# Compressive memory of 32 heads as 32x32 blocks of head pairs, with q and k rows ordered pair by pair

## The chip, the cores and the metric

The kernel runs on one core of a Trainium2 chip. It uses five instruction engines: PE (TensorE, the matmuls; PEld is its weight load), DVE (VectorE), ACT (ScalarE), POOL (GpSimd) and SP (SyncE, which here does nothing but issue DMAs, in the order of the program). The metric is the device time of one execution in microseconds. Three executions of the kernel before took 783.08, 779.81 and 781.45 us, median 781.45 us.

## What is computed

One transformer block on x of 2048 rows and 512 features, with a LayerNorm whose scale and shift come from a condition vector ahead of each half. The first half is an attention with 32 heads of 16 features that walks over four segments of 512 rows; inside a segment it is causal softmax attention, and across segments each head carries a 16x16 memory matrix M and a 16-vector z. The second half is a feed-forward net (512 to 1792 to 512, GELU). The part that the change touches, cut from the reference:

```python
phi = lambda t: jnp.where(t > 0, t + 1.0, jnp.exp(t))
for s in range(N):                       # N = 4 segments
    qs, ks, vs = q[:, :, s], k[:, :, s], v[:, :, s]
    logits = jnp.einsum("bhqd,bhkd->bhqk", qs, ks) * scale + mask
    a_dot = jnp.einsum("bhqk,bhkd->bhqd", _softmax(logits, axis=-1), vs)
    pq = phi(qs)
    num = jnp.einsum("bhld,bhde->bhle", pq, M)
    den = jnp.einsum("bhld,bhd->bhl", pq, z)[..., None] + 1e-6
    outs.append(g * num / den + (1.0 - g) * a_dot)
    pk = phi(ks)
    M = M + jnp.einsum("bhld,bhle->bhde", pk, vs)
    z = z + jnp.einsum("bhld->bhd", pk)
```

## The kernel before

Everything is float32. Where a product has to run at the fast rate, an operand is split into a high and a low part in the reduced type (f32r) and the product takes three matmuls.

The program has three stages. **Projections** (0 to about 177 us of the profiled span): for each segment s = 0 to 3 the normalised rows are transposed (`a_turn`, line 160, names At), scaled (ACT, Ah), split by DVE into Ahh and Ahl (lines 138 and 139), and multiplied by wq, wk and wv: four groups of 128 feature rows for q (12 matmuls of 128x512 each, line 334), four for k, and four blocks of 128 rows for v (12 matmuls each, line 485). **Attention** (to about 475 us): for each head, S units (line 649) whose masked maximum DVE takes (line 637), T units (line 723), exponentials on ACT, and products with V (line 751). **Feed-forward net** (to the end). The first S and T units start while v of segment 3 is still being projected.

The order of the work in the projections is written by hand, as a list of tokens for each segment (`PRM['A']`), and no scheduler changes it. Q0 to Q3, K0 to K3 and V0 to V3 are the projections; R is `mem_read`, U `mem_update`, Ro and Rz `mem_out`, Rs `mem_store`, Rb `mem_load`, At, Ah and H make the next segment's transposed and split input, Tk and Tc transpose the rows of phi(k) and copy them out, and B fills the first two stacks (below). The list of segment 2 reads:

```python
'Q0 Ro s0 D D Q1 s1 D D Q2 s2 Q3 E s3 r K0 Es p0 K1 El p1 K2 p2 K3 R V0 p3 V1 Rs V2 Rb Tk Tc V3 At Ah H U Rn'
```

Segment 1 has the same shape, segment 0 has no R, and segment 3 ends with "... K2 R K3 Rz Rs" and has no U. All PSUM tiles of this stage (`pst`) come in turn from one pool of eight banks, so that a matmul also waits for the last reader of the tile that was allocated eight tiles earlier.

**A group** is 128 feature rows of q or k, which are 8 heads of 16 features. `head_rows` permutes the columns of wq and wk so that row r of a group is feature r // 8 of head r % 8. The heads of a group are thus interleaved, and a product of two heads that don't belong together has to be masked away.

**The memory.** `mem_update` (token U) forms, for each group g, the full 128x128 product of phi(k) and v over the segment's 512 rows: 16 matmuls of 128x128 (line 434, tile mp), of which the mask `mbd` keeps one eighth (line 440), and adds M of the segment before (line 443). `mem_read` (token R) forms the denominators with four matmuls of 32 columns (line 449, tile dn), their reciprocal on DVE (lines 451 to 453, tile rd), and the numerators with four matmuls of 128x512, one per group (line 457, tiles nu), each copied from PSUM by ACT into a tile am (line 459). `mem_store` (line 465) writes rd to DRAM, `mem_load` reads it back broadcast (rb), POOL multiplies am by rb, and `mem_out` (line 480) writes the four am tiles of a segment to DRAM (AMD). In segment 3 the am tiles are written unmultiplied.

**The stacks.** `proj` leaves each group's q or k as two f32r parts in SBUF, and `store` (line 502) writes them to DRAM: the part that is needed twice as one DMA of 512 KB with a broadcast source, the other as one of 256 KB. QD and KD are laid out as [part 3, feature 16, head 8, 512]. `load_stacks` (line 193) reads them back, two heads at a time, as 48 rows (3 parts by 16 features) of 1024 numbers, which lie 16 KB apart in DRAM: for a quarter of heads, Q, two loads for k (kst) and two for q (qst). The first two Q are loaded by token B, in segment 3.

**Queues.** All of these DMAs are issued by SP, strictly in the order of the program. Each DMA waits for one of eight completion semaphores (DMAHW0 to DMAHW7, taken in turn), that is, for the landing of the DMA eight before it on SP's list, beside the waits for its data.

Of the kernel before, what the change touches and what calls it, by code (L numbers as in the profile page):

```python
# [8 lines left out]
F32 = mybir.dt.float32  # L9
# [3 lines left out]
ALU = mybir.AluOpType  # L13
# [9 lines left out]
VW = 17  # L23
# [81 lines left out]
def block_kernel(ctx: ExitStack, tc: tile.TileContext, x, wq, wk, wv, wo, betaq, betam,  # L105
# [56 lines left out]

    QD = [[dram.tile([3, 16, 8, 512], F32, name=f"QD{s}_{g}") for g in range(4)] for s in range(NSEG)]
    KD = [[dram.tile([3, 16, 8, 512], F32, name=f"KD{s}_{g}") for g in range(4)] for s in range(NSEG)]
    TERMS = {"q": (slice(0, 3, 2), slice(1, 2)), "k": (slice(0, 2), slice(2, 3))}
    def home(Q):
# [19 lines left out]
    def load_stacks(Q):  # L186
        s, g, t = Q // 8, (Q // 2) % 4, Q % 2
        for st, dd in ((kst[home(Q)], KD), (qst[home(Q)], QD)):
            rows = dd[s][g].rearrange("c r e n -> (c r) e n")
            for h in range(2):  # L190
                o = 4 * t + 2 * h
                if len(st) == 3:
                    sp.dma_start(st[2][64 * h:64 * h + 48], rows[:, o:o + 2, :])
                else:
                    for p in range(2):
                        sp.dma_start(st[p][64 * h:64 * h + 48], rows[:, o + p, :])
# [26 lines left out]
    with ExitStack() as pa:  # L223
# [4 lines left out]
        def pst(name):  # L228
            return pp.tile([128, 512], F32, tag="ps", name=name)
# [47 lines left out]
        load_x(1)  # L277
        mbd = wp.tile([128, 128], F32, name="mbd")
        m8 = wp.tile([128, 32], F32, name="m8")
# [146 lines left out]
        def mem_update(s):  # L426
            z = zss[s]
            if mem["z"] is not None:
                v.tensor_tensor(out=z, in0=mem["z"], in1=z, op=ALU.add)
            mp = pst(f"mp{s}")  # L430
            for g in range(4):
                for b in range(4):
                    rhs = V[4 * s + b][:, VW * 8 * g:VW * 8 * g + VW * 8].rearrange("p (h c) -> p h c", c=VW)[:, :, :16]
                    pe.matmul(mp[:, 128 * g:128 * g + 128], pks[s][b][:, 128 * g:128 * g + 128], rhs,
                              start=(b == 0), stop=(b == 3))
# [4 lines left out]
            v.tensor_tensor(out=M, in0=mp.rearrange("p (g n) -> p g n", g=4),  # L440
                            in1=mbd[:, :].unsqueeze(1).to_broadcast([128, 4, 128]), op=ALU.mult)
            if mem["M"] is not None:
                v.tensor_tensor(out=M, in0=M, in1=mem["M"], op=ALU.add)
            mem["M"], mem["z"], mem["zm"] = M, z, zm

        def mem_read(s):
            dn = pst(f"dn{s}")
            for g in range(4):
                pe.matmul(dn[32 * g:32 * g + 32, :], mem["zm"][:, g, :], phq[s, g], start=True, stop=True)
            rd = sa.tile([128, 512], F32, tag="rd", bufs=1, name=f"rd{s}")  # L450
            v.tensor_scalar(rd, dn, 1e-6, None, op0=ALU.add)
            v.reciprocal(out=rd, in_=rd)
            v.tensor_scalar(rd, rd, gm[:, 0:1], None, op0=ALU.mult)
            ams = []
            for g in range(4):
                ps = pst(f"nu{s}_{g}")
                pe.matmul(ps, mem["M"][:, g, :], phq[s, g], start=True, stop=True)
                am = sat("am" if s < 3 else "phk", f"am{s}_{g}")
                act.activation(am, ps, AF.Copy)
                ams.append(am)  # L460
            mrd[s] = [rd, ams, []]

        def mem_store(s):
            rdd = dram.tile([128, 512], F32, name=f"rdd{s}")
            sp.dma_start(rdd, mrd[s][0])
            mrd[s][0] = mem["r"] = rdd

        def mem_load(s):
            for g in range(4):
                rb = sat("pkt", f"rb{s}_{g}")  # L470
                sp.dma_start(rb, mrd[s][0][32 * g:32 * g + 8, :].unsqueeze(1).to_broadcast([8, 16, 512]))
                mrd[s][2].append(rb)
# [5 lines left out]
        def mem_out(s):  # L478
            for g, am in enumerate(mrd[s][1]):
                sp.dma_start(AMD[s][g], am)  # L480

# [973 lines left out]
```

## Time and profile before

| what | before |
|---|---|
| median of three executions | 781.45 us (779.81 to 783.08) |
| the execution with the profile | 786.26 us |
| its span in the trace | 784.5 us |
| busy, DVE | 564.9 us (72%) |
| busy, ACT | 456.6 us (58%) |
| busy, POOL | 258.1 us (33%) |

The span runs from the first to the last instruction of the trace; the 1.8 us between it and the execution's own time lie before and behind it. Every position below, such as "at 80 us", counts from the start of the span. In the trace a float32 matmul of the program appears as two records, so the 16 matmuls of `mem_update` are 32 records on PE.

### The profile page before, as it was taken

How to read it: one execution, taken by the hardware profiler on the slowest of the kernel's cores; microseconds unless marked ns; L12 is line 12 of the kernel's file. 1: busy time of each engine (PE TensorE's matmuls, PEld its weight loads, DVE VectorE, ACT ScalarE, POOL GpSimd, SP SyncE). 2: the span in 40 equal slices, each digit the busy share in tenths (PEclk: the TensorE clock that was granted, in tenths of full speed). 3: DMA queues.
4: the chain of work that ended last, by engine and by line, in shares of the span. 5: the costliest groups of instructions: out<-in, count | busy, mean ns of one | idle time of the engine just before them, and what ended most of it. 6: DMA issues, size and time to landing. Idle time of an engine off the chain costs nothing.

```text
span 784.5 us, 14474 instructions
## 1 busy us (share of the span) xinstructions
PE 773.5 (99%) x4532; PEld 541.2 (69%) x4532; DVE 564.9 (72%) x1686; ACT 456.6 (58%) x918; POOL 258.1 (33%) x437
## 2 busy tenths in 40 slices
PE   9999999999999999999999999999999999999998
PEld 4887787866555445555555547788878888888887
DVE  6765696449999889999988889868569764432424
ACT  3543444443888667777788676767644446652221
POOL 2205143410468445566665662242000404200000
PEclk9999999999999779999999999999999999999999
DMA  9777755396587677878777755595676524545543
GB/s 337 268 258 262 281 213 200 144 315 196 136 195 183 164 169 185 228 206 228 185 201 209 214 167 158 195 303 177 201 232 207 191 94 163 173 147 167 172 127 115
DMA packets 97376, 156.28 MB, mean 199 GB/s; under 512 B 15552, under 2 KB 31296, under 8 KB 97300
## 3 DMA queue, kind: packets, MB, share of 16 engines
q1 hardware_dynamic: 96436, 153.79, 63.6%
q10 hardware_dynamic: 864, 1.57, 0.6%
q8 instruction: 36, 0.59, 0.3%
q14 instruction: 40, 0.33, 0.1%
HBM read 93.95 MB, written 60.83 MB: 197 GB/s over the span
## 4 chain that ended last, share of the span: by engine, by line
PE 83%; DVE 5%; DMA 5%; ACT 3%; issue 2%; SPq 1%; POOL 0%; ACTq 0%; DVEq 0%; POOLq 0%
PE bx L1102 9%; PE att L723 8%; PE pv L751 7%; PE att L649 5%; PE q L334 5%; PE bx L1372 5%; PE bv L1102 5%; PE k L334 5%; PE by L1372 4%; PE bv L1372 4%; PE v L485 4%; PE mm L839 4%; PE spare L1372 2%; PE by L1102 2%; PE mm L751 2%
## 5 line engine op out<-in xcount | busy, mean ns | idle before, releaser
L637 DVE CUSTOM_DVE_ANT_0 dump<-att,maskb 128x512 bf16<-128x512 f32 (+3 forms) x512 | 220.2, 487 | 22.5 <-PE att L649 12.9
L723 PE MATMUL att<-qst,kst 50*128 50x512 f32 (+3 forms) x512 | 137.2, 378 | 2.6 <-DVE nm L637 2.2
L649 PE MATMUL att<-kst,qst 48*128 48x512 f32 (+3 forms) x512 | 122.7, 352 | 0.1
L723 PEld LDWEIGHTS att<-qst,kst 50*128 50x128 f32 x512 | 79.5, 191 | 62.1 <-DVE nm L637 47.6
L649 PEld LDWEIGHTS att<-kst,qst 48*128 48x128 f32 x512 | 77.7, 192 | 19.5 <-ACT ptc L726 8.5
L726 ACT ACTIVATE pta<-att 128x512 f32<-128x512 f32 x128 | 69.2, 592 | 32.2 <-PE att L723 25.1
L726 ACT ACTIVATE ptb<-att 128x384 f32<-128x384 f32 x128 | 62.9, 492 | 23.8 <-PE att L649 18.2
L883 POOL TENSOR_TENSOR wb<-wa 128x256 f32<-128x256 f32 x24 | 20.3, 847 | 152.4 <-DMA wa<-in_w 152.4
L708 POOL TENSOR_SCALAR_AFFINE_SELECT pta<-pta 128x256 f32<-128x256 f32 x64 | 27.2, 425 | 104.2 <-ACT pta L726 102.4
L726 ACT ACTIVATE ptc<-att 128x384 f32<-128x384 f32 x128 | 57.2, 492 | 0.9 <-PE att L723 0.9
L139 DVE TENSOR_TENSOR gl<-s,gh 128x512 fp32r<-128x512 f32 x34 | 24.1, 708 | 43.0 <-ACT gh L136 42.9
L708 POOL TENSOR_SCALAR_AFFINE_SELECT ptc<-ptc 128x256 f32<-128x256 f32 x128 | 52.0, 422 | 1.6 <-ACT ptc L726 0.5
L136 ACT ACTIVATE gh<-s 128x512 fp32r<-128x512 f32 x34 | 21.3, 628 | 47.7 <-DMA s<-GD 15.9
L1107 ACT ACTIVATE s<-s,b1t 128x512 f32<-128x512 f32 x42 | 30.3, 722 | 21.5 <-DVE s L1111 21.5
L1111 DVE TENSOR_TENSOR s<-bv,s 128x512 f32<-128x512 f32 x28 | 19.3, 689 | 32.1 <-PE bv L1102 22.3
L637 DVE DVE_READ_ACCUMULATOR2_ANT nm<- 128x1 f32 x512 | 42.2, 82 | 0.0
L708 POOL TENSOR_SCALAR_AFFINE_SELECT ptb<-ptb 128x256 f32<-128x256 f32 x64 | 26.9, 420 | 34.7 <-ACT ptb L726 34.7
L520 POOL TENSOR_SCALAR qp<-qp 128x512 f32<-128x512 f32 x12 | 18.5, 1546 | 42.9 <-ACT qp L515 42.9
L751 PE MATMUL pv<-pta,V 128*32 128x512 f32 x208 | 29.4, 639 | 0.5 <-ACT ms L130 0.5
L139 DVE TENSOR_TENSOR w1ml<-s,w1mh 128x512 fp32r<-128x512 f32 x18 | 13.0, 720 | 21.9 <-ACT w1mh L136 21.9
L751 PE MATMUL pv<-ptc,V 128*32 128x256 f32 (+1 forms) x416 | 28.1, 344 | 0.0
L136 ACT ACTIVATE w1mh<-s 128x512 fp32r<-128x512 f32 x18 | 11.3, 629 | 26.0 <-PE spare L1372 11.6
(378 smaller groups left out, 2078.7 us busy)
## 6 DMA issues: line engine op xcount, KB each, us to landing
GD<-s SPq DMA_DIRECT2D x56, 256.0 KB
s<-GD SPq DMA_DIRECT2D x52, 256.0 KB
kst<-KD SPq DMA_DIRECT2D x58, 192.0 KB
qst<-QD SPq DMA_DIRECT2D x58, 192.0 KB
QD<-q SPq DMA_DIRECT2D x16, 512.0 KB
KD<-k SPq DMA_DIRECT2D x16, 512.0 KB
TD<-ts SPq DMA_DIRECT2D x32, 256.0 KB
xt<-X2D SPq DMA_DIRECT2D x28, 256.0 KB
```

The source lines that it names most:

```text
L136: act.activation(hi, src, AF.Copy)
L139: lo_eng.tensor_tensor(out=lo, in0=src, in1=hi.bitcast(F32), op=ALU.subtract)
L334: pe.matmul(ps, a[:, k, 128 * g:128 * g + 128], b[k], start=(k == 0 and i == 0), stop=(k == KB - 1 and i == 2))
L485: pe.matmul(ps, a[k][:, 128 * b:128 * b + 128], w[:, k, :], start=(k == 0 and i == 0), stop=(k == KB - 1 and i == 2))
L637: v.tensor_tensor_reduce(out=dump[n_dump[0] % 2][:, :n], in0=src, in1=maskb[:, 512 - n:], scale=-1.0, scalar=-4 * NEG, op0=ALU.add, op1=AL ...
L649: pe.matmul(ps[:, o:o + n], q[:, 128 * i:128 * i + 128], k[:, :n], start=True, stop=True)
L708: pool.affine_select(out=t, in_=t, pattern=pattern, compare_op=ALU.is_ge, fill=0.0, base=0, channel_multiplier=-1)
L723: pe.matmul(ps[:, o:o + n], k[:, 128 * j:128 * j + 128], q[:, 128 * j:], start=True, stop=True)
L726: act.activation(pt[:, h, :], ps[:, :m], AF.Exp, scale=0.25)
L751: pe.matmul(ps[32 * c:32 * c + 32, lo:hi], V[4 * s + j][:, VW * hd:VW * hd + 32], pt[:, c // 2, lo - o:hi - o], start=start, stop=stop)
L1102: pe.matmul(ps, a[:, i, k, :], b[k], start=start and k == 0 and c == 0, stop=k == 1 and c == 2, skip_group_check=not start)
L1372: pe.matmul(ps, a[:, c], w[:, lo:hi], start=(f == 0 and i == 0), stop=(last and i == 2))
```

## The change

The row order in a group becomes pair by pair: 32 rows hold two heads, row 2 f + e of them being feature f of head e of the pair. The block of M that matters is then the 32x32 block on the diagonal of each pair, and only these are formed. In `mem_update` 16 matmuls of 128x128 become 64 of 32x32, each still over the 128 rows of one block b; in `mem_read` four matmuls of 128x512 become 16 with 32 rows and 32 columns by 512, placed by `tile_position`, and the tiles nu now hold pair r of all four groups instead of group g. The four PSUM banks of nu are allocated ahead of the matmuls, and ACT copies them after all sixteen. `mbd`, M and the two DVE operations on M shrink to a quarter.

The DRAM layout becomes [pair 4, feature 16, part 3, head 2, 512]. A load of two heads reads one contiguous piece of 192 KB, again as 48 rows of 1024; a store becomes three DMAs of 256 KB with runs of 4 KB at a distance of 12 KB, where it was one of 512 KB and one of 256 KB. AMD is one tile per segment, into which each am goes as four blocks of 32 rows; rd of segments 0 to 2 goes out as four DMAs of 16 KB instead of one of 256 KB. Which instructions ACT and POOL execute, and in which order, does not change.

```diff
-    QD = [[dram.tile([3, 16, 8, 512], F32, name=f"QD{s}_{g}") ...
+    QD = [[dram.tile([4, 16, 3, 2, 512], F32, name=f"QD{s}_{g}") ...
-    TERMS = {"q": (slice(0, 3, 2), slice(1, 2)), "k": (slice(0, 2), slice(2, 3))}
+    TERMS = {"q": ((0, 2), (1,)), "k": ((0, 1), (2,))}
...
     def load_stacks(Q):
-            rows = dd[s][g].rearrange("c r e n -> (c r) e n")
             for h in range(2):
-                o = 4 * t + 2 * h
+                rows = dd[s][g][2 * t + h].rearrange("r c e n -> (r c) e n")
                 if len(st) == 3:
-                    sp.dma_start(st[2][64 * h:64 * h + 48], rows[:, o:o + 2, :])
+                    sp.dma_start(st[2][64 * h:64 * h + 48], rows)
...
-    AMD = [[dram.tile([128, 512], F32, name=f"AMD{s}_{g}") for g in range(4)] for s in range(NSEG)]
+    AMD = [dram.tile([4, 128, 512], F32, name=f"AMD{s}") for s in range(NSEG)]
...
             for g in range(4):
                 for b in range(4):
-                    rhs = V[4 * s + b][:, VW * 8 * g:VW * 8 * g + VW * 8].rearrange("p (h c) -> p h c", c=VW)[:, :, :16]
-                    pe.matmul(mp[:, 128 * g:128 * g + 128], pks[s][b][:, 128 * g:128 * g + 128], rhs,
-                              start=(b == 0), stop=(b == 3))
+                    for r in range(4):
+                        h = VW * (8 * g + 2 * r)
+                        rhs = V[4 * s + b][:, h:h + 2 * VW].rearrange("p (h c) -> p h c", c=VW)[:, :, :16]
+                        pe.matmul(mp[32 * r:32 * r + 32, 32 * g:32 * g + 32],
+                                  pks[s][b][:, 128 * g + 32 * r:128 * g + 32 * r + 32], rhs, start=(b == 0), stop=(b == 3))
...
-            M = sa.tile([128, 4, 128], F32, tag="M", name=f"M{s}")
+            M = sa.tile([128, 4, 32], F32, tag="M", name=f"M{s}")
...
+            nu = [pst(f"nu{s}_{r}") for r in range(4)]
             for g in range(4):
-                ps = pst(f"nu{s}_{g}")
-                pe.matmul(ps, mem["M"][:, g, :], phq[s, g], start=True, stop=True)
-                am = sat("am" if s < 3 else "phk", f"am{s}_{g}")
+                for r in range(4):
+                    pe.matmul(nu[r][32 * g:32 * g + 32, :], mem["M"][32 * r:32 * r + 32, g, :], phq[s, g][32 * r:32 * r + 32, :],
+                              start=True, stop=True, tile_position=(32 * r, 32 * g))
+            for r, ps in enumerate(nu):
+                am = sat("am" if s < 3 else "phk", f"am{s}_{r}")
                 act.activation(am, ps, AF.Copy)
...
         def mem_store(s):
-            rdd = dram.tile([128, 512], F32, name=f"rdd{s}")
-            sp.dma_start(rdd, mrd[s][0])
+            if s < 3:
+                rdd = dram.tile([4, 4, 2, 512], F32, name=f"rdd{s}")
+                for g in range(4):
+                    sp.dma_start(rdd[:, g], mrd[s][0][32 * g:32 * g + 8, :])
+            else:
...
         def mem_out(s):
-            for g, am in enumerate(mrd[s][1]):
-                sp.dma_start(AMD[s][g], am)
+            for r, am in enumerate(mrd[s][1]):
+                sp.dma_start(AMD[s][:, 32 * r:32 * r + 32, :], am)
...
         def store(parts, nm, dd):
-            rows = dd.rearrange("c r e n -> (r e) c n")
-            for t, c in zip(parts, TERMS[nm]):
-                d = rows[:, c]
-                sp.dma_start(d, t.bitcast(F32).unsqueeze(1).to_broadcast([128, d.shape[1], 512]))
+            rows = dd.rearrange("t r c e n -> (t r) c e n")
+            for t, cs in zip(parts, TERMS[nm]):
+                for c in cs:
+                    sp.dma_start(rows[:, c], t.bitcast(F32))
```

The first place is SP's list in segment 3, from the last store of K2 to the loads of the third stack (kst and qst, line 193 before, 192 after); am is a numerator tile, rd the reciprocal, k a part of K3. Before:

```order
L502 DMA KD_2_103<-k_2_1818 128x512 [waits DMAHW7_49,DVE_49]
L480 DMA AMD_0_117<-am_0_1834 128x512 [waits DMAHW0_49,Activation_49]
L480 DMA AMD_1_118<-am_1_1838 128x512 [waits DMAHW1_49,Activation_49]
L480 DMA AMD_2_119<-am_2_1842 128x512 [waits DMAHW2_49,Activation_49]
L480 DMA AMD_3_120<-am_3_1846 128x512 [waits DMAHW3_49,Activation_49]
L465 DMA rdd_1871<-rd_1828 128x512 [waits DMAHW4_49,DVE_49]
L502 DMA KD_3_104<-k_3_1861 128x2x512 [waits DMAHW5_49,Activation_49]
L502 DMA KD_3_104<-k_3_1862 128x512 [waits DMAHW6_49,DVE_49]
L193 DMA kst_1949<-KD_1_90 48x1024 [waits DMAHW7_49,PE_49,Activation_49]
L193 DMA kst_1949<-KD_1_90 48x1024 [waits DMAHW0_49,Activation_49]
L193 DMA qst_1948<-QD_1_74 48x1024 [waits DMAHW1_49]
L193 DMA qst_1948<-QD_1_74 48x1024 [waits DMAHW2_49]
```

After:

```order
L489 DMA AMD_108<-am_0_2044 4x32x512 [waits DMAHW5_49,Activation_49]
L489 DMA AMD_108<-am_1_2046 4x32x512 [waits DMAHW6_49,Activation_49]
L489 DMA AMD_108<-am_2_2048 4x32x512 [waits DMAHW7_49,Activation_49]
L489 DMA AMD_108<-am_3_2050 4x32x512 [waits DMAHW0_49,Activation_49]
L474 DMA rdd_2076<-rd_2020 128x512 [waits DMAHW1_49,DVE_49]
L511 DMA KD_3_104<-k_3_2065 64x2x512 [waits DMAHW2_49,Activation_49]
L511 DMA KD_3_104<-k_3_2065 64x2x512 [waits DMAHW3_49]
L511 DMA KD_3_104<-k_3_2066 64x2x512 [waits DMAHW4_49,DVE_49]
L192 DMA kst_2155<-KD_1_90 48x1024 [waits DMAHW5_49,PE_49,Activation_49]
L192 DMA kst_2155<-KD_1_90 48x1024 [waits DMAHW6_49,Activation_49]
L192 DMA qst_2154<-QD_1_74 48x1024 [waits DMAHW7_49]
L192 DMA qst_2154<-QD_1_74 48x1024 [waits DMAHW0_49]
```

The store of K3 has three rows instead of two, and the first load of the stack, whose semaphore was that of the last store of K2 (DMAHW7), now waits on that of the first am tile (DMAHW5): the loads wait for the landing of the four am stores.

The second place is PE in segment 1, from the last denominators to the first matmul of v (token R, then V0). Before:

```order
L449 MATMUL dn_1038<-qp_3_930,zm_813 32x512 [waits DVE_49]
L457 MATMUL nu_0_1047<-qp_0_835,M_818 128x512
L457 MATMUL nu_1_1051<-qp_1_860,M_818 128x512
L457 MATMUL nu_2_1055<-qp_2_891,M_818 128x512
L457 MATMUL nu_3_1059<-qp_3_930,M_818 128x512 [waits DVE_49]
L485 MATMUL v_0_1063<-wvh,Ahh_0_780 128x512 [waits DVE_49]
```

After (the rows between are those for groups 1 and 2, alike):

```order
L450 MATMUL dn_1089<-qp_3_976,zm_857 32x512 [waits DVE_49]
L459 MATMUL nu_0_1098<-qp_0_879,M_862 32x512
L459 MATMUL nu_1_1099<-qp_0_879,M_862 32x512
L459 MATMUL nu_2_1100<-qp_0_879,M_862 32x512
L459 MATMUL nu_3_1101<-qp_0_879,M_862 32x512 [waits DVE_49]
...
L459 MATMUL nu_0_1098<-qp_3_976,M_862 32x512
L459 MATMUL nu_1_1099<-qp_3_976,M_862 32x512
L459 MATMUL nu_2_1100<-qp_3_976,M_862 32x512
L459 MATMUL nu_3_1101<-qp_3_976,M_862 32x512
L494 MATMUL v_0_1126<-wvh,Ahh_0_776 128x512 [waits DVE_49]
```

Four rows become sixteen in the same place, each writing 32 rows of its bank; the wait for the fourth bank stands at the fourth row.

The third place is PE at the end of segment 1, where `mem_update` is followed by Q0 of segment 2 (pk are the transposed rows of phi(k), one for each of the four row blocks b). Before, for the first group and the last matmul:

```order
L434 MATMUL mp_1212<-V_199,pk_0_1145 128x128 [waits Activation_49]
L434 MATMUL mp_1212<-V_200,pk_1_1147 128x128
L434 MATMUL mp_1212<-V_201,pk_2_1149 128x128 [waits Activation_49]
L434 MATMUL mp_1212<-V_202,pk_3_1151 128x128 [waits Activation_49]
...
L434 MATMUL mp_1212<-V_202,pk_3_1151 128x128
L334 MATMUL q_0_1241<-Ahh_0_1195,wqh 128x512 [waits DVE_49]
```

After:

```order
L435 MATMUL mp_1279<-V_187,pk_0_1212 32x32 [waits Activation_49]
L435 MATMUL mp_1279<-V_187,pk_0_1212 32x32 x3
L435 MATMUL mp_1279<-V_188,pk_1_1214 32x32 x4
L435 MATMUL mp_1279<-V_189,pk_2_1216 32x32 [waits Activation_49]
L435 MATMUL mp_1279<-V_189,pk_2_1216 32x32 x3
L435 MATMUL mp_1279<-V_190,pk_3_1218 32x32 [waits Activation_49]
L435 MATMUL mp_1279<-V_190,pk_3_1218 32x32 x3
...
L333 MATMUL q_0_1356<-Ahh_0_1262,wqh 128x512 [waits DVE_49]
```

Each row of before becomes four in its place; Q0 still follows directly and still waits for DVE's split of the new input.

More of the change, by code (lines that the diff above doesn't have):

```diff
@@ L161, in turned @@
         return ps
[L163 to L165 removed]
+    QD = [[dram.tile([4, 16, 3, 2, 512], F32, name=f"QD{s}_{g}") for g in range(4)] for s in range(NSEG)]
+    KD = [[dram.tile([4, 16, 3, 2, 512], F32, name=f"KD{s}_{g}") for g in range(4)] for s in range(NSEG)]
+    TERMS = {"q": ((0, 2), (1,)), "k": ((0, 1), (2,))}
     def home(Q):
@@ L277, in block_kernel @@
         load_x(1)
-        mbd = wp.tile([128, 128], F32, name="mbd")
+        mbd = wp.tile([128, 32], F32, name="mbd")
         m8 = wp.tile([128, 32], F32, name="m8")
@@ L463, in mem_store @@
         def mem_store(s):
-            rdd = dram.tile([128, 512], F32, name=f"rdd{s}")
-            sp.dma_start(rdd, mrd[s][0])
+            if s < 3:
[3 more added lines that the diff above has]
+            else:
+                rdd = dram.tile([128, 512], F32, name=f"rdd{s}")
+                sp.dma_start(rdd, mrd[s][0])
             mrd[s][0] = mem["r"] = rdd
         def mem_load(s):
-            for g in range(4):
-                rb = sat("pkt", f"rb{s}_{g}")
-                sp.dma_start(rb, mrd[s][0][32 * g:32 * g + 8, :].unsqueeze(1).to_broadcast([8, 16, 512]))
+            for r in range(4):
+                rb = sat("pkt", f"rb{s}_{r}")
+                sp.dma_start(rb, mrd[s][0][r].rearrange("g h n -> (g h) n").unsqueeze(1).to_broadcast([8, 16, 512]))
                 mrd[s][2].append(rb)
@@ L1425 @@
     row = np.arange(128)
-    head_of_row = row % 8
+    head_of_row = 2 * (row // 32) + row % 2
     a = {
```

10 lines of the change are left out of this document (5 added, 5 removed).

## The prediction

> **What bounds the kernel now.** I read the page first: the busy times and the chain that ended last, by engine.
>
> ```profile
> span 784.5 us, 14474 instructions
> PE 773.5 (99%) x4532; PEld 541.2 (69%) x4532; DVE 564.9 (72%) x1686; ACT 456.6 (58%) x918; POOL 258.1 (33%) x437
> PE 83%; DVE 5%; DMA 5%; ACT 3%; issue 2%; SPq 1%; POOL 0%; ACTq 0%; DVEq 0%; POOLq 0%
> ```
>
> PE is nearly always busy and carries 83% of the chain, so PE work that goes can shorten the span, but only where nothing else arrives later. Next I read the chain in order of time (start, length, what) for the pieces that the change makes smaller, and segment 3, where it leaves PE.
>
> ```profile
> 52.70 3.57 PE mp L434 x32
> 80.42 0.99 PE dn L449 x8
> 81.41 3.63 PE nu L457 x8
> 99.52 3.57 PE mp L434 x32
> 127.08 3.63 PE nu L457 x8
> 145.19 3.57 PE mp L434 x32
> ...
> 158.64 1.06 ACT kst L181
> ...
> 160.99 6.44 DMA QD<-q
> ...
> 167.53 0.61 ACT k L516
> ...
> 168.85 0.61 DVE qp L526
> ...
> 169.50 1.05 PE dn L449 x2
> 170.55 3.63 PE nu L457 x8
> 174.18 2.76 PE k L334 x12
> ```
>
> All three mp and all three nu lie on the chain: 3 x 3.57 + 3 x 3.63 = 21.6 us, the most that both together could give. In segment 3 a store of q is on it for 6.44 us: K0 needs the buffer that the store frees. What is saved at each place is limited by what is late next, so I take the six places one by one.
>
> **nu in segments 1 and 2.** A numerator goes from 4 matmuls (8 records) to 16 (32 records). The denominators show the price of column tiles: 8 records of 512 columns take 0.99 us, where 8 of nu take 3.63, so the four tiles of 32 columns run side by side. Rows can run side by side too:
>
> ```profile
> 192.18 0.51 PE L649 MATMUL att<-kst,qst 48*128 48x512 f32 x2
> ```
>
> Two matmuls of 48 rows, in the upper and the lower half of the array, take 0.51 us together. A record of nu costs 3.63 / 8 = 0.454 us now. If all sixteen tiles run side by side, nu is 32 x 0.454 / 16 = 0.9 us; if only the column tiles do, 32 x 0.99 / 8 = 4.0. I take 1.2, near the rows on which both kinds of tile are seen side by side, so PE is free 2.4 us earlier. What is late then is the third block of v (V2), which takes the PSUM bank of K3, and DVE frees that with line 526, behind the long reciprocal:
>
> ```profile
> 84.83 3.35 DVE L452 RECIPROCAL rd<-rd 128x512 f32<-128x512 f32 x1
> 88.62 0.68 DVE L526 SCALAR_TENSOR_TENSOR kp<-k,kp 128x512 f32<-128x512 f32 x1
> 90.35 0.39 PE L485 MATMUL v<-wvh,Ahh 128*128 128x512 f32 x1
> 133.30 0.68 DVE L526 SCALAR_TENSOR_TENSOR kp<-k,kp 128x512 f32<-128x512 f32 x1
> 136.03 0.39 PE L485 MATMUL v<-wvh,Ahh 128*128 128x512 f32 x1
> ```
>
> DVE doesn't move, since it starts from dn, which stays. Segment 1: the bank is free at 89.3, V2 starts at 90.35, so **1.1** of the 2.4 us remain. Segment 2: free at 134.0, V2 at 136.03, so **2.1** remain. With nu at 4.0 both are zero, or a loss of 0.4 each.
>
> **mp.** It becomes 64 matmuls, 128 records of 32x32. If column tiles run side by side as in dn, 128 x (0.99 / 8) x (32 / 512) = 1.0 us; if they run one after the other and a record costs by its columns, 128 x (3.57 / 32) / 4 = 3.57, as now; if a record costs what it costs now, 14.3. I take up to 3.3, near the shortest records of the trace:
>
> ```profile
> L751 PE MATMUL att<-ptc,V x16: 272/326/379, 475.2 to 475.7; 128*32 128x128 f32 x8, 128*32 128x256 f32 x8
> ```
>
> Sixteen of them, on four column tiles, start within 0.5 us: 0.03 us each, with more columns than mp has. What follows mp, Q0, gains almost nothing from any length below that. It multiplies Ahh and Ahl as fast as DVE splits them (pairs: the last split, and PE's matmul that needs it):
>
> ```profile
> 58.92 0.69 DVE L139 TENSOR_TENSOR Ahl<-Ah,Ahh 128x512 fp32r<-128x512 f32 x1
> 59.67 0.50 PE L334 MATMUL q<-Ahl,wqh 128*128 128x512 f32 x1
> 104.50 0.69 DVE L139 TENSOR_TENSOR Ahl<-Ah,Ahh 128x512 fp32r<-128x512 f32 x1
> 105.46 0.40 PE L334 MATMUL q<-Ahl,wqh 128*128 128x512 f32 x1
> 148.55 0.69 DVE L139 TENSOR_TENSOR Ahl<-Ah,Ahh 128x512 fp32r<-128x512 f32 x1
> 151.13 0.39 PE L334 MATMUL q<-Ahl,wqh 128*128 128x512 f32 x1
> 142.53 2.52 POOL L476 TENSOR_TENSOR am<-am,rb 128x512 f32<-128x512 f32 x2 [0.47 <-DMA rb<-rdd]
> 100.35 1.65 DVE L139 TENSOR_TENSOR Ahl<-Ah,Ahh 128x512 fp32r<-128x512 f32 x1
> ```
>
> After segment 0 PE uses the split at once (0.06 us), after segment 1 it has 0.27 us to gain, after segment 2 up to 1.9. But in segment 2 the split now starts 2.1 us earlier, while POOL still multiplies am by rb until 145.1, and beside such a multiplication a split took 1.65 us in segment 1 instead of 0.69. I put 1.5 us of that against the 1.9: **0.4** in all, between 0 and 1.9.
>
> **Segment 3: loads and the q store.** The loads of the first two stacks read rows that lie 16 KB apart; after the change they read one piece. Windows (us, busy of PE, PEld, DVE, ACT, POOL, then PE's granted clock, share of the 16 DMA engines, GB/s):
>
> ```profile
> 161.00:165.00 4.00, 4.00 (x20) 3.30 (x19) 2.32 (x4) 0.78 (x2) 2.34 (x2) 1.00 1.02 213
> 167.50:173.00 5.50, 4.82 (x16) 1.53 (x15) 2.97 (x5) 2.78 (x5) 0.00 (x0) 1.00 1.05 406
> 0.00:20.00 20.00, 18.27 (x75) 9.40 (x76) 13.96 (x37) 7.87 (x14) 4.20 (x41) 1.00 0.93 338
> 178.00:200.00 22.00, 22.00 (x112) 14.09 (x112) 21.06 (x103) 9.80 (x18) 1.59 (x4) 1.00 0.50 149
> ```
>
> With the engines full, these loads move 213 GB/s, the stores behind them 406, and the loads of whole rows at the start 338 / 0.93 = 363. Eight loads of 192 KB take 1.57 MB / 213 = 7.4 us, at 363 they take 4.3. The q store is queued behind them and would land up to **3.1** us earlier; bounds 0 and 3.1, and I take the upper end, as its rate is that of the only other big loads on full engines. K0, DVE's chain to dn, and nu follow it. From 178 us DVE is the engine in front (21.06 of 22 us busy), and it has the reciprocal of segment 3 behind dn, so the 2.4 us of the third nu give PE time that it can't use; I take **0.4**, between 0 and 2.4.
>
> **The am stores.** Each now goes out as 4 blocks of 32 rows. What a DMA with few slow-moving blocks costs is shown by rb, whose source has 8 rows, and in SP's list by the place of these stores:
>
> ```profile
> 137.00:140.50 3.50, 3.50 (x26) 3.14 (x25) 0.00 (x0) 1.55 (x4) 1.27 (x1) 1.00 0.51 190
> 173.15 3.07 SPq L480 DMA_DIRECT2D AMD<-am  x4
> 178.81 1.59 SPq L193 DMA_DIRECT2D kst<-KD x2
> 180.46 0.92 SPq L193 DMA_DIRECT2D qst<-QD x2
> ```
>
> Four rb loads, alone, fill half of the engines (0.51). By that, four blocks fill a quarter: 95 GB/s, and 1.05 MB of am takes 11.0 us instead of the 2.6 at 406. The loads of the third stack wait for these landings. Issued 3.5 us earlier, near 169.7, the am stores end near 181.5. Only then can the last of the loads be issued, and a DMA behind full engines took up to 6.44 us to land (the q store above): between 187 and 190 with the issue. The first S unit that needs them, at 192.18 above, is then due at 188.7. I put **+1.0**, between 0 (the blocks spread as now) and +2.5.
>
> **What I cost at nothing.** 32 more store DMAs, about 0.46 us of SP each by the row at 180.46: bytes and order stay, and full engines (share 1.05) hide the issue; without this cover segment 3 would lose 8 x 0.46 = 3.7 us. Four small rd stores for one: rb is late by up to 1 us, and only POOL waits for it. M, at a quarter of the columns, saves DVE time where PE doesn't wait.
>
> **Sum.** -1.1 - 2.1 - 0.4 - 3.1 - 0.4 + 1.0 = -6.1 us: the span goes from 784.5 to 778.4, the profiled execution from 786.26 to 780.2. That execution lies 4.8 us over the median of 781.45; against the median it is **775.3 us**.
>
> **Rivals.** (1) *The stack loads stay slow.* They write only 48 rows of each half of a tile, and the rate could come from that. Then the 3.1 goes and, as the S units are due later, the +1.0 may go too: -3.0 to -4.0, and a little less where segment 3 waits for DMA anyway; **778.5**. For it: no row shows such a load from contiguous memory. (2) *Row tiles don't run side by side.* nu stays near 4 us: -0.4 - 3.1 + 1.0 = -2.5, **779**. Against it stands the row at 192.18. (3) *mp becomes longer: a record has a floor.* It is on the other side. The loss begins above 4.8 us after segment 0 (Q0 has 1.2 us of slack to DVE there), 3.6 after segment 1 and 3.3 after segment 2. At T us a record it is 3 x 128 T - 11.7; to be over 0.5% slower against the other terms of -5.7 it needs 0.056 us, which is half of what a record costs now (3.57 / 32 = 0.112): **785.5**; at 0.112 it loses 31.3, **807**. Against it stands the 0.03 above. The Trainium skill, "TensorE: Matmul & The Clock Gate", section "Wait — 56ns, not 53.3ns?", gives about 25 ns from start to start however small the matmul, or about 62 ns for each MATMUL where the sequencer's software decodes it; an estimate by that page is 3.2 us for mp, which leaves the sum as it is, or 7.9, which makes it 787.9; the 0.03 us a record of this trace speaks against the second. (4) *The am stores stall more*, +2.5 instead of +1.0: **776.8**. (5) *The change does less than it says*, since neither wait of V2 nor the split allows it: with (1) and (2) together **781**.
>
> **How the numbers follow.** Forecast, (4) included: 0.48. (1): 0.22. (2): 0.10. (5): 0.07. (3): 0.13, of which 0.11 is over the bound; 0.02 more for the store DMAs without their cover, out of (5). 0.5%, or 3.9 us, is about what a measurement of this kernel can tell from no change, so faster means under 777.5: the forecast's own range is 771.5 (mp after segment 2 and the third nu at their upper ends) to 777.8, and (1) lies on the bound. Faster 0.50, most of the forecast and a small part of (1); same 0.37; slower 0.13. The range of 8 in 10 reaches from 771 to 784, which takes in (1), (2), (5) and the mild part of (3).
>
> **What would show it.** nu near 1.2 us and mp below 3.3 in the chain; V2 directly behind line 526 in segment 1; the loads of the first two stacks at over 300 GB/s on full engines, and the q store off the chain or shorter; the share of the DMA engines near 0.25 while the am stores run, and the third stack's first S unit waiting for a DMA or not. Records of mp at over 0.05 us, or a stack load as slow as now, would make the prediction wrong.

## The result and the profile after

The changed kernel takes a median of 790.91 us (789.3 to 793.06, 4 runs), the kernel before 782.27 in the same comparison: a ratio of 1.0116, 95% interval 1.0079 to 1.0153. That is 8.6 us slower, where 6 us faster had been forecast, and outside the range of 771 to 784. Executions that lie more than 1.5% above the fastest of their kernel, at a lower granted clock, are left out of all ratios here but not of the medians; e4 had one such of 4, and e6, e7, e8, e11 and e12 had 3, 4, 2, 3 and 2 of 10, so a ratio and two medians need not agree. The profiled execution took 791.53 us, with a span of 789.8. The page, the same three lines as before:

```profile
span 789.8 us, 15250 instructions
PE 767.9 (97%) x4892; PEld 536.0 (68%) x4892; DVE 567.3 (72%) x1686; ACT 455.3 (58%) x918; POOL 256.6 (32%) x437
PE 76%; DMA 8%; DVE 8%; issue 4%; ACT 3%; SPq 1%; ACTq 0%; DVEq 0%
```

PE lost 5.6 us of busy time and 7 points of the chain; DMA and DVE took most of them over. The chain in order of time (start, length, what) says where:

```profile
52.52 1.11 PE mp L435 x96
53.62 1.75 issue
...
80.46 1.00 PE dn L450 x8
81.45 1.16 PE nu L459 x32
...
127.79 1.14 PE nu L459 x32
...
169.94 1.07 PE nu L459 x32
171.90 2.06 PE k L333 x9
...
174.61 1.03 ACT kst L181
175.64 13.74 DMA AMD<-am
189.40 5.13 DMA qst<-QD
```

The matmuls did what the change wanted: mp went from 3.57 us to 1.1, nu from 3.63 to 1.16. But a store of am, which nobody reads for over 100 us, now stands on the chain for 13.74 us, followed by a load of the third stack that had to wait for it. PE's rows at that place (start, length, instruction, idle time before it and what ended it):

```profile
190.65 0.40 PE L494 MATMUL pv<-wvl,Ahh 128*128 128x512 f32 x1
193.83 0.46 PE L658 MATMUL att<-kst,qst 48*128 48x512 f32 x1 [2.79 <-DMA qst<-QD]
194.62 0.47 PE L658 MATMUL att<-kst,qst 48*128 48x512 f32 x2 [0.33 <-DMA qst<-QD]
```

PE stood still for 3.1 us. The windows of the changed kernel (us, busy of PE, PEld, DVE, ACT, POOL, PE's granted clock, share of the DMA engines, GB/s), at the stack loads, at the am stores (two windows, the second inside the first), and behind the wait:

```profile
161.00:165.00 4.00, 4.00 (x19) 3.34 (x18) 1.96 (x4) 0.42 (x1) 1.97 (x2) 1.00 0.96 240
175.00:182.00 7.00, 6.41 (x29) 3.89 (x29) 6.96 (x26) 2.32 (x3) 0.00 (x0) 1.00 0.52 178
177.00:179.00 2.00, 1.41 (x5) 0.50 (x3) 2.00 (x8) 0.00 (x0) 0.00 (x0) 1.00 0.25 92
196.00:216.00 20.00, 20.00 (x77) 12.11 (x78) 10.99 (x55) 8.37 (x20) 3.68 (x9) 0.50 0.27 62
```

and of the kernel before, for the longer window at the am stores and for the last one:

```profile
175.00:182.00 7.00, 7.00 (x33) 4.62 (x32) 6.57 (x22) 2.71 (x3) 0.00 (x0) 1.00 1.05 406
196.00:216.00 20.00, 20.00 (x161) 11.02 (x161) 19.18 (x91) 16.65 (x40) 8.33 (x21) 1.00 0.56 135
```

While am is stored, half of the DMA engines' time goes unused (0.52 against 1.05), in the middle of it three quarters (0.25), and for 20 us behind PE's wait the granted clock is 0.50: PE is busy all the time and gets through 77 matmul records instead of 161. In the kernel before, the first S unit starts at 176.9 us and the first product with V at 204.1, 27.2 us later; here at 173.9 and 213.4, 39.5 later. A lead of 3.0 us became an arrear of 9.3.

The profiled execution of before lost some of its own time to the clock later on, which is why the two profiles are only 5.3 us apart while the medians are 8.6: its window from 240 to 280 us (the first row) has 0.83, that of the changed kernel (the second) has 1.00.

```profile
240.00:280.00 40.00, 39.65 (x304) 18.91 (x301) 34.39 (x161) 30.73 (x74) 22.64 (x43) 0.83 0.66 173
240.00:280.00 40.00, 39.54 (x354) 20.33 (x348) 39.07 (x189) 34.84 (x87) 28.77 (x54) 1.00 0.72 180
```

What nu saved in segments 1 and 2 was lost there already. DVE's splits of the next input, and POOL's multiplications, in the changed kernel:

```profile
96.40 2.71 POOL L485 TENSOR_TENSOR am<-am,rb 128x512 f32<-128x512 f32 x2 [16.30 <-ACT V L498]
98.00 1.66 DVE L139 TENSOR_TENSOR Ahl<-Ah,Ahh 128x512 fp32r<-128x512 f32 x1
104.31 0.69 DVE L139 TENSOR_TENSOR Ahl<-Ah,Ahh 128x512 fp32r<-128x512 f32 x1
143.65 1.67 DVE L139 TENSOR_TENSOR Ahl<-Ah,Ahh 128x512 fp32r<-128x512 f32 x1
145.01 2.85 POOL L485 TENSOR_TENSOR am<-am,rb 128x512 f32<-128x512 f32 x2 [0.25 <-issue]
149.84 0.69 DVE L139 TENSOR_TENSOR Ahl<-Ah,Ahh 128x512 fp32r<-128x512 f32 x1
```

The splits begin 2.2 us earlier after segment 1 (96.90 against 99.11) and 1.6 earlier after segment 2, but the last of the row of eight starts at 104.31 (104.50 before) and 149.84 (148.55 before). Beside POOL a split of 0.69 us takes 1.66, and DVE ends hardly earlier (0.2 us) after segment 1 and later (1.3 us) after segment 2. PE, which waits for the splits, then also loses clock (0.66 from 103 to 108 us, 1.00 before); e3 and e6 below bear on both.

### The profile page after: what moved, and what is told of

It is laid out like the page before. It is cut to its first block, busy times and chain, and to the rows that moved or that the text cites. A ratio compares the mean times of both kernels' runs of the same rounds, so it can differ in the third digit from the quotient of the medians.

```text
span 789.8 us, 15250 instructions
## 1 busy us (share of the span) xinstructions
PE 767.9 (97%) x4892; PEld 536.0 (68%) x4892; DVE 567.3 (72%) x1686; ACT 455.3 (58%) x918; POOL 256.6 (32%) x437
## 4 chain that ended last, share of the span: by engine, by line
PE 76%; DMA 8%; DVE 8%; issue 4%; ACT 3%; SPq 1%; ACTq 0%; DVEq 0%
PE bx L1111 9%; PE att L732 7%; PE pv L760 6%; PE bx L1381 5%; PE q L333 5%; PE by L1381 5%; PE bv L1381 5%; PE bv L1111 5%; PE k L333 5%; PE v L494 4%; PE att L658 4%; PE mm L848 3%; PE spare L1381 2%; DVE dump L646 2%; PE by L1111 2%
## 5 line engine op out<-in xcount | busy, mean ns | idle before, releaser
L658 PE MATMUL att<-kst,qst 48*128 48x512 f32 (+3 forms) x512 | 124.8, 356 | 3.8 <-DMA qst<-QD 3.1
L1116 ACT ACTIVATE s<-s,b1t 128x512 f32<-128x512 f32 x42 | 30.3, 722 | 21.9 <-DVE s L1120 21.8
L1120 DVE TENSOR_TENSOR s<-bv,s 128x512 f32<-128x512 f32 x28 | 19.3, 688 | 30.3 <-PE bv L1111 21.4
L333 PE MATMUL q<-Ahh,wqh 128*128 128x512 f32 x64 | 27.2, 425 | 2.8 <-DVE Ahh L138 2.8
L333 PE MATMUL q<-Ahl,wqh 128*128 128x512 f32 x64 | 26.9, 421 | 1.5 <-DVE Ahl L139 1.5
```

Of the source, the lines that this page charges most:

```text
L333: pe.matmul(ps, a[:, k, 128 * g:128 * g + 128], b[k], start=(k == 0 and i == 0), stop=(k == KB - 1 and i == 2))
L658: pe.matmul(ps[:, o:o + n], q[:, 128 * i:128 * i + 128], k[:, :n], start=True, stop=True)
L1116: act.activation(dst, src, AF.Gelu_apprx_tanh, bias=b1t[:, f:f + 1])
```

## The experiments

Three causes were on the table: the am stores on few DMA engines, the clock behind the wait, and the collision of DVE and POOL; beside them the loads, which should have become faster, and the third store DMA. Starts of the first S unit and of the first product with V are from each trace; ratios are to the kernel before, run in the same comparison (its median was 780.5 to 782.3 us there).

| run | median us | ratio, 95% interval | first S | first product with V |
|---|---|---|---|---|
| before | 782.27 | 1 | 176.9 | 204.1 |
| changed kernel | 790.91 | 1.0116 [1.0079, 1.0153] | 173.9 | 213.4 |
| e1: am whole | 798.65 | 1.0206 [1.0166, 1.0245] | 177.2 | 207.5 |
| e2: layout only | 780.64 | 1.0003 [0.9968, 1.0037] | 177.3 | 204.5 |
| e3: e1 and dummies | 796.34 | 1.0181 [1.0117, 1.0244] | 172.4 | 201.3 |
| e4: e1 and later multiplications | 795.86 | 1.0143 [1.0069, 1.0217] | 168.4 | 202.8 |
| e5: e1 and loads in pieces | 782.44 | 1.0023 [0.9997, 1.0048] | 174.6 | 203.5 |
| e6: e5 and later multiplications | 776.56 | 0.9929 [0.9905, 0.9954] | 167.8 | 199.5 |
| e7: e6 and dummies | 784.27 | 1.0017 [0.9986, 1.0047] | 170.8 | 202.5 |
| e8: before, later multiplications | 784.75 | 1.0016 [0.9984, 1.0048] | 176.6 | 205.4 |
| e9: change, wait filled | 784.49 | 1.0057 [1.0036, 1.0079] | 176.9 | 210.2 |
| e10: e5 and rows of 2 KB | 783.4 | one execution | 177.7 | 206.7 |
| e11: am whole in segment 3 | 781.4 | 0.9983 [0.9954, 1.0012] | 177.0 | 205.9 |
| e12: before, am in blocks | 789.62 | 1.0078 [1.0047, 1.0108] | 177.8 | 214.3 |

The positions are those of one execution each. Up to the first S unit the changed kernel, e1, e5, e9 and e11 differ only in how am is stored, and that unit lies between 173.9 and 177.2 us in them; a difference of 3 us in this column alone says little. The stretch between the two columns depends on it less.

**e1, am stored whole.**

```diff
-                sp.dma_start(AMD[s][:, 32 * r:32 * r + 32, :], am)
+                sp.dma_start(AMD[s][r], am)
...
-                sp.dma_start(am, AMD[U // 4][U % 4])
+                sp.dma_start(am, AMD[U // 4][:, 32 * (U % 4):32 * (U % 4) + 32, :])
```

> The changed kernel, but each am tile is stored as one piece of 128 rows (AMD keeps pair r in front), and the loads of the attention stage read four blocks of 32 rows instead. Theory A: the four am stores of segment 3 ran on a quarter of the DMA engines and held up the third stack's loads; PE then stood still near 190 us and its clock was halved from 196 to 216. Then here the 13.74 us wait for AMD leaves the chain, the share of the DMA engines right after 173 us is near 1, no half clock follows, and the time is 776 to 779 us. Rival B: the stall came from the third store DMA of K3 and the semaphores in turn, or from slower loads of the stacks; then the third stack is still late by over 4 us and the time stays over 787.

The wait went, as theory A says: first product with V 30.3 us behind the first S unit instead of 39.5. The time didn't follow; it rose to 798.65. The edit had moved the four blocks from the stores to the loads of the attention stage, and there another DMA now waits (chain, start, length):

```profile
292.48 7.42 DMA qst<-ms
```

From the start of the first product with V to that of the last, e1 takes 271.2 us (207.5 to 478.7), the changed kernel 262.4 (213.4 to 475.8). This run therefore couldn't decide; e5 does.

**e5, the loads in pieces too.**

```diff
+                for r in range(4):
+                    sp.dma_start(am[32 * r:32 * r + 32], AMD[U // 4][r, 32 * (U % 4):32 * (U % 4) + 32, :])
```

> As the run with whole am stores, but each of the twelve am loads of the attention stage is four loads of 32 rows, so that neither the stores nor the loads have a slowest dimension of 4. Theory A (few DMA engines, at whichever end): the losses of that run behind 290 us (+3 to +13 against the kernel before) go, and the time is 779 to 783 us, some 8 to 10 under the changed kernel and 15 to 18 under that run. Rival: the attention stage lost there because of PE's clock or the store and load lanes, not the loads of four blocks: then the time stays over 790.

782.44 us, ratio 1.0023: all of the loss is gone, with the same bytes as in e1 and 36 loads more; against the changed kernel only the shape of the am stores and loads differs. The window at the am stores is full again:

```profile
175.00:182.00 7.00, 6.43 (x29) 3.82 (x27) 6.96 (x24) 3.00 (x4) 0.00 (x0) 1.00 1.05 405
```

**e11, whole only in segment 3.**

```diff
+                sp.dma_start(AMD[s][:, 32 * r:32 * r + 32, :] if s < 3 else AMD[s][r], am)
```

> The changed kernel with am stored whole in segment 3 alone (and its four loads at the end of the attention stage in four pieces of 32 rows each); segments 1 and 2 store their am in four blocks as in the changed kernel. Theory A says that only the stores of segment 3 stand ahead of loads that somebody waits for: the time is that of the run with whole stores and pieces, 780 to 784 us. Rival: the stores of segments 1 and 2 delay q and k too, and the time stays over 786.

781.4 us: the stores of segments 1 and 2 may stay in blocks. It is the place that costs, ahead of loads that PE waits for.

**e12, the cost alone, added to the kernel before.**

```diff
+    AMB = [dram.tile([4, 48, 512], F32, name=f"AMB{g}") for g in range(4)]
...
-                sp.dma_start(AMD[s][g], am)
+                sp.dma_start(AMD[s][g] if s < 3 else AMB[g][:, :32, :], am)
```

> The kernel before, with one thing added: the four am stores of segment 3 go out as four blocks of 32 rows into a padded tile, and are loaded at the end of the attention stage in four pieces of 32 rows. Everything else, the memory's matmuls, the row order, the loads of the stacks, is as before. Theory A: the four DMA engines alone make the loss; the third stack is late by 4 to 8 us, PE waits, the clock is halved near 195 to 215 us, and the time is 786 to 794 us. Rival: in the kernel before, whose first S unit is 3 us later, the loads have time enough, or the third store of K3 was part of it; then it stays within 2 us of the kernel before.

789.62 us, ratio 1.0078: four DMAs out of some 700 make about two thirds of the loss by the ratios (0.78% of 1.16%) in a kernel that has nothing else of the change, and the stretch from the first S unit to the first product with V grows from 27.2 to 36.5 us (39.5 in the changed kernel). Its windows and PE's wait:

```profile
175.00:182.00 7.00, 7.00 (x33) 4.62 (x31) 6.51 (x16) 3.31 (x4) 0.00 (x0) 1.00 0.57 210
196.00:216.00 20.00, 20.00 (x73) 11.62 (x72) 11.77 (x56) 8.33 (x19) 3.67 (x9) 0.51 0.21 49
194.62 0.47 PE L650 MATMUL att<-kst,qst 48*128 48x512 f32 x1 [1.43 <-DMA qst<-QD]
```

Here PE's wait is only 1.43 us (and 0.31 behind it), and the clock halves all the same.

**e9, the wait stays, but PE is kept busy in it.**

```diff
+            if (P, z, h) == (4, "a", 0):
+                for _ in range(20):
+                    pe.matmul(ps, maskb[:, :128], maskb, start=True, stop=True)
```

> The changed kernel with twenty dummy matmuls of 128x512 in bf16 (about 4.4 us of PE) ahead of the first S unit of the third stack, into the bank that this unit then overwrites; the wait for the am stores stays. Theory E: PE's wait of some 3 us is what halves the clock from 196 to 216, and of the 13.6 us that the changed kernel loses between 177 and 206 us about 8 are the clock. Then here the third stack is as late as there (first S unit of it near 194), but no half clock follows and the time is 782 to 786 us. Rival: the loss is the wait itself and what it does to DVE and the later loads; then the time stays within 2 us of 790.9.

784.49 us, 6.4 under the changed kernel for 4.5 us of useless matmuls, and the window that was at 0.50 is at full clock (the third stack's first unit starts only at 198.35 us, since the dummies last longer than the wait did):

```profile
193.93 4.49 PE L656 MATMUL att<-maskb 128*128 128x512 bf16 x19
196.00:216.00 20.00, 20.00 (x138) 11.30 (x135) 16.51 (x79) 11.72 (x29) 5.46 (x14) 1.00 0.45 106
```

So in the traces, of the 12.3 us that the changed kernel loses between the first S unit and the first product with V (39.5 against 27.2), some 6 are the clock: here the stretch is 33.3. In e5, where nothing is late, it is 28.9, since DVE can't start as early as PE; the remaining 4 to 5 are the wait. The totals give e9 less by the ratios (1.0057 against 1.0116, or 4.6 us) than by the medians, so the share of the clock is good to 2 us or so.

**e2, the layout without the blocks.** The row order, layout, loads and three stores of the change with the memory of before:

```diff
-            nu = [pst(f"nu{s}_{r}") for r in range(4)]
...
+                ps = pst(f"nu{s}_{g}")
+                pe.matmul(ps, mem["M"][:, g, :], phq[s, g], start=True, stop=True)
...
-                sp.dma_start(AMD[s][:, 32 * r:32 * r + 32, :], am)
+                sp.dma_start(AMD[s][g], am)
```

> Row order, DRAM layout, contiguous stack loads and three stores as in the changed kernel; memory update and read, am and rd stores as in the kernel before (16 matmuls of 128x128 with a mask, 4 of 128x512). Theory A with faster loads: nothing stalls, the stack loads of segment 3 pass 300 GB/s on full engines, the first S unit is 3 us earlier than before: 778 to 780 us. Rival 1: contiguous loads are no faster, and the layout alone leaves the time at 781 to 784. Rival B: the third store DMA costs time by itself: over 785.

780.64 us, ratio 1.0003: rival 1, if 0.4 us under its range. The contiguous loads run no faster than the strided ones did (208 GB/s, 213 before), and the third store costs nothing:

```profile
161.00:165.00 4.00, 4.00 (x19) 3.34 (x18) 2.48 (x4) 1.10 (x3) 2.65 (x2) 1.00 1.02 208
```

**e10, rows of 2 KB**, for the rate of the first two stacks' loads:

```diff
-                if len(st) == 3:
+                if len(st) == 3 and Q > 1:
```

> As the run with whole stores and pieces, but the loads of the first two stacks (segment 3) take each head by itself, 48 rows of 2 KB, sixteen loads instead of eight. Theory F: the rate of 208 to 213 GB/s belongs to rows of 4 KB; then the engines pass 300 GB/s here while these loads run alone. Rival G: it belongs to the few rows (48 partitions) that each load writes; then it stays at 190 to 230 GB/s with the engines full.

With the engines full and only loads under way, the window shows

```profile
166.00:168.00 2.00, 2.00 (x11) 1.65 (x10) 0.00 (x0) 0.00 (x0) 0.00 (x0) 1.00 1.06 190
```

Neither the distance of the rows nor their length is the reason. Of the reasons considered, that each load writes only 48 partitions is left; it wasn't tried by itself, so the cause stays open. One execution took 783.4 us.

**e4 and e6, the multiplications later.**

```diff
- 'Q0 Ro s0 D D Q1 s1 D D Q2 s2 Q3 E s3 ... V3 At Ah H U Rn'
+ 'Q0 Rm s0 D D Q1 s1 D D Q2 s2 Q3 Ro E s3 ... V3 At Ah H U'
- 'Q0 Ro Q1 B Q2 Q3 K0 ...'
+ 'Q0 Rm Q1 B Q2 Q3 Ro K0 ...'
```

> As the run with whole am stores, with POOL's multiplications of am by rb moved from the end of a segment behind Q0 of the next, and the am stores behind Q3. Theory D: in the changed kernel the multiplications run beside DVE's splits of the next input, which then take 1.1 to 1.7 us each instead of 0.4 and 0.7, and this eats what nu saved in segments 1 and 2; then the splits are short again here, dn of segment 3 starts 2.5 to 4 us earlier than in that run, and the time is 772 to 776. Rival: the splits are slow for another reason (PE or ACT feeds them late): within 1 us of that run.

> The same with POOL's multiplications moved behind Q0 of the next segment and the am stores behind Q3. In the run with that move the first S unit came 8.5 us earlier than before, then the lead shrank to 1 us by 200 us while the clock was halved. Theory D: first S unit again 7 to 9 us earlier than before; time 777 to 780 us. Rival: DVE and the clock take all of it back, time within 1.5 us of the run without the move.

In e4 the first S unit comes at 168.4, 8.8 us before that of e1, but the time, 795.86 us where 772 to 776 had been expected, can't be told from e1's (the intervals overlap): the loads in blocks of e1 are still there. With whole stores and pieces (e6) the time is **776.56 us, ratio 0.9929 [0.9905, 0.9954]: faster than both kernels**, 5.9 us under e5 by the medians and 0.94% by the ratios, from this move alone. Its DVE and POOL rows after segment 1:

```profile
97.20 0.69 DVE L139 TENSOR_TENSOR Ahl<-Ah,Ahh 128x512 fp32r<-128x512 f32 x1
100.39 0.69 DVE L139 TENSOR_TENSOR Ahl<-Ah,Ahh 128x512 fp32r<-128x512 f32 x1
103.81 5.95 POOL L485 TENSOR_TENSOR am<-am,rb 128x512 f32<-128x512 f32 x4
```

The splits are at 0.69 us throughout and end 3.9 us earlier than in the changed kernel. Of the 9.1 us of lead at the first S unit 4.6 are left at the first product with V. DVE, busy for 9.87 of the 10 us there, is late with its reciprocal and the maxima, PE waits, and the clock falls again:

```profile
168.00:178.00 10.00, 8.02 (x26) 4.66 (x25) 9.87 (x28) 3.95 (x6) 0.00 (x0) 0.83 1.06 397
```

**e8, the same move in the kernel before.**

> The kernel before, with only the same move of the multiplications and of the am stores. Theory D says that the collision with the splits belongs to segments in which the splits start while POOL still multiplies: in the kernel before it is there in segment 1 only (about 2.2 us), so dn of segment 3 comes 1 to 2.5 us earlier and the time is 779 to 781 us. Rival: the moved work is in the way of K or of the stack loads instead: 782 us or more.

784.75 us, ratio 1.0016: no gain, against theory D's 779 to 781 us, and no loss either. An explanation, not shown, would be that the splits of before, behind a longer nu and mp, collide in segment 1 alone and have time; together with e6 the run shows only that the move pays with the short matmuls and not without them.

**e3 and e7, dummy matmuls behind mp.**

```diff
+            for _ in range(10):
+                pe.matmul(mp[:, 128:], maskb[:, :128], maskb[:, :384], start=True, stop=True)
```

> As the run with whole am stores, with ten dummy matmuls of 128x384 in bf16 behind each mp, into columns of its bank that nobody reads, so that PE isn't idle while DVE splits the next input. Theory C: the half clock at 55.8 to 59.2 and at 103.6 to 107 us came from that idle time and cost a part of what mp and nu saved; then it is gone here and the time is 1.5 to 3 us under that run. Rival: Q0 is paced by DVE in any case and the clock there costs nothing: within 1 us of that run.

> The same with the ten dummy matmuls behind each mp. Theory C: no half clock ahead of 200 us but for the start, and 1 to 3 us under the run without them; rival: no difference over 1 us, since the clock falls again where PE waits for DVE at the start of the attention stage.

e3 is 2.3 us under e1, but the intervals overlap: inconclusive. The traces say more. From 103 to 108 us, in e1 and in e3:

```profile
103.00:108.00 5.00, 3.56 (x8) 2.30 (x9) 4.20 (x11) 1.31 (x3) 2.38 (x3) 0.64 0.38 144
103.00:108.00 5.00, 4.84 (x18) 3.22 (x19) 4.46 (x14) 1.70 (x3) 1.49 (x1) 1.00 0.16 57
```

The dummies keep the clock up, while splits beside POOL stay slow (1.64 us). dn of segment 3 then starts at 166.66 us, against 167.40 in the changed kernel, whose last split of segment 1 starts within 0.3 us of that of e3: there the half clock cost less than 1 us. In e1 dn starts at 171.20, after a longer half clock and a collision that took another course, and one execution can't separate the two. In e6, where the splits are short and the same window is at 1.00 without dummies, dn starts at 160.07.

e7 is slower than e6 (1.0017 against 0.9929, intervals apart). Once the splits are short, PE has no idle time to fill behind mp of segments 1 and 2 (in e6 it is busy for all of the 5 us from 103 and the 8 us from 148), and the dummies only stand ahead of Q0 there.

## Why the prediction was wrong

- **mp and nu, in size: right.** Forecast 1.0 to 3.3 us and 1.2; measured 1.1 and 1.16. By group (busy time, mean ns and idle time before them, of all three segments; the first two rows are of before, the last two of the changed kernel) PE has 14.6 us less to do:

```profile
L434 PE MATMUL mp<-V,pk 128*128 128x128 f32 x96 | 11.2, 275 | 0.0
L457 PE MATMUL nu<-qp,M 128*128 128x512 f32 x24 | 11.1, 605 | 0.0
...
L435 PE MATMUL mp<-V,pk 128*32 128x32 f32 x384 | 4.1, 198 | 1.8 <-issue 1.8
L459 PE MATMUL nu<-qp,M 32*32 32x512 f32 x96 | 3.6, 599 | 0.0
```

  Row and column tiles do run side by side, so rival 2 falls, and with 1.1 us for 128 records rival 3 as well.
- **The floor per matmul.** The Trainium skill, page "TensorE: Matmul & The Clock Gate", section "Wait — 56ns, not 53.3ns?", gives about 25 ns from start to start however small the matmul, or about 62 ns where the sequencer's software decodes it. The 128 records of mp start within 1.15 us, 9 ns apart. The measurement decides: neither figure holds between tiles that lie side by side.
- **The am stores: the step that failed.** It was put at "+1.0, between 0 and +2.5". The mechanism was the right one, the quarter of the engines included (0.25 and 92 GB/s from 177 to 179 us; 95 had been forecast); its size was off by two things. The wait was longer. The step has the am stores issued near 169.7 us and landed near 181.5; SP issued them from 173.54 us, as the 3.5 us that were to bring them forward weren't there, and behind K's stores; the last landed at 189.4 (175.64 + 13.74). The loads were issued from 183.66 to 189.7 us and not near 182, with the rd store and K3's three stores between, which wait for landings too:

```profile
173.54 2.78 SPq L489 DMA_DIRECT2D AMD<-am  x4
176.55 2.85 SPq L474 DMA_DIRECT2D rdd<-rd  x1
179.49 4.06 SPq L511 DMA_DIRECT2D KD<-k  x3
183.66 2.47 SPq L192 DMA_DIRECT2D kst<-KD  x2
186.18 3.53 SPq L192 DMA_DIRECT2D qst<-QD  x2
```

  The third stack's first S unit, due at 188.7 us by the step, came at 193.83. And the price of a wait was taken as the wait itself. Up to the first product with V it was 10.6 us (39.5 against the 28.9 of e5), of which e9 puts some 6 on the clock that halves behind the wait. e5 and e11 show that the loss goes with these stores, e12 that they make most of it alone.
- **The loads: the second step that failed.** "I take the upper end, as its rate is that of the only other big loads on full engines" was the choice between 0 and 3.1. e2 measured 208 GB/s with contiguous rows, so the term is 0. (In the changed kernel the window shows 240 at a share of 0.96, but q's stores were issued from 160.95 us on, inside it; the q store on its chain landed at 166.8 us, 0.6 before the 167.4 of before.) Rival 1 was right, at 0.22.
- **nu in segments 1 and 2.** The gain up to the transposes was 2.2 us in segment 1 (At at 95.40 against 97.61), so the limit of 1.1 by V2 wasn't there: V2 started at 88.14, before DVE freed the bank that the step named (88.55). But the collision of the splits with POOL, which the prediction charged 1.5 us in segment 2 alone, was there in both, and with the clock that falls behind PE's idle time it took nearly all of it: dn of segment 3 starts 0.4 us earlier than before. e6 gives it back, 5.9 us of the total; it takes away the collision and the half clock together. e3, which takes away the half clock alone, has dn at 166.66 us and e6 at 160.07, so the collision is the larger part.
- **nu in segment 3: right.** It was put at 0.4 of 2.4 us, since DVE is in front there. In e5 the first S unit is 2.3 us earlier than before and the first product with V about half a us.
- **The rest of the sum.** Without the am stores' wait the forecast was -7.1 us. e5, which has no such wait, is at 1.0023 [0.9997, 1.0048]: none of it arrived.
- **At nothing:** 32 more stores, and the rd stores, cost nothing that e2 or e5 could show. That was right.
- **The rivals.** The forecast's slower case was mp's length. What happened was rival 4, "the am stores stall more", at over three times its price (8.5 us between the changed kernel and e5), with a consequence (the clock) that no part of the sum contained.

## What to carry to other kernels

Look at the outermost dimension of both sides of every new DMA, and at what stands behind it in its queue: a store that nobody waits for can hold up a load that everybody waits for. On a stretch where PE is the bound, a wait of 2 or 3 us can cost more than double, because the clock may fall behind it, so count both. And when PE gets faster at one place, ask which two other engines now work at the same time that didn't before: here the gain came only after POOL's work had been moved away from DVE's.

## What the runs showed that was not expected

- Small tiles start very close together: 128 records of 128x32 in 1.35 us in the changed kernel, the last one's own length (0.2 us) included, so about 9 ns from one to the next.

```profile
143.53 1.35 PE L435 MATMUL mp<-V,pk 128*32 128x32 f32 x128
```

- A wait of PE of 3.1 us (in e12 of 1.7 us) among otherwise busy rows is followed by some 20 us at a granted clock of 0.50. In e9, with the same loads late but PE busy, it isn't. Not every such wait does it: behind one of 2.00 us in e10 the clock stays at 1.00. What decides between them stays open.

```profile
172.71 1.05 PE L450 MATMUL dn<-qp,zm 128*32 128x512 f32 x2 [2.00 <-DVE qp L535]
172.00:176.00 4.00, 3.29 (x39) 1.42 (x40) 2.15 (x5) 2.03 (x4) 0.00 (x0) 1.00 1.05 402
176.00:180.00 4.00, 4.00 (x19) 2.57 (x17) 3.93 (x3) 3.26 (x6) 0.00 (x0) 1.00 1.03 382
```

- Loads of 48 partitions move 190 to 213 GB/s on full engines, whether their rows are 4 KB at 16 KB distance, contiguous, or 2 KB; stores on full engines move 405.
- A DVE split takes 1.66 us instead of 0.69 beside a POOL multiplication of the same size.
